# Unread products of ones in TensorE's planned waits, and other prices in the planner, in a clustered attention and feed-forward kernel

## The chip, the cores and the metric

The kernel runs on one core of a Trainium2 chip. The metric is the device time of one execution in microseconds (us). Three executions before the change took 919.37, 920.08 and 920.59 us, so the median is 920.08 us.

## The reference

Inputs: `q`, `k`, `v` of shape (4 batches, 8 heads, 768 positions, 64), 16 centroids per head, `moe_w_in` (512 x 2048), `moe_w_out` (2048 x 512), all float32. For each batch and head every query and key is given to the centroid whose normalised product with it is largest; a query attends only to keys of its own cluster:

```
mask   = q_assign[:, :, :, None] == k_assign[:, :, None, :]
scores = where(mask, scale * q @ k.T, -1e9)
attn   = softmax(scores);  attn_out = attn @ v
x = attn_out as 3072 tokens x 512
h = x @ w_in
g = where(h >= 1, h, where(h <= -1, 0, (h + 1)**2 / 4))
out = g @ w_out                       # 3072 x 512
```

## The kernel before, in words

Float32 operands are scaled and split into two float16 parts (high and low), and a product is three float16 products (high by high, high by low, low by high). Heads go in pairs: `kv_load` brings q, k and v of a pair, `kv_scale`, `kq_split`, `v_split` and `assign` scale, split, transpose (by DMA) and find the clusters. A batch has three units of 256 query rows; for every unit and head pair there are four score tiles of 128 rows by 768 keys. `at_scores` makes one (8 matmuls of 384 columns) in a pair of PSUM banks, VectorE adds a term and takes the row minimum into `sS` and `sbi`, ScalarE takes the exponential (`at_soft`), and the result is split into high and low and transposed: early in the run, every second tile by 6 TensorE transposes against the identity `idf` (`by_tensor`), otherwise by GpSimd, ScalarE and a DMA transpose (`hl` to `pT`). `at_av` multiplies by v: 8 small and 36 large matmuls of 64 output rows in the bank `bank_a`, which only `at_av` writes; ScalarE copies one half of that bank, VectorE reads the other, and the unit's `x` results. `ffn1` (24 matmuls of 256 columns) and `ffn2` (12 of 512 columns) are the feed-forward part, for 8 slices of the hidden width. The two weight matrices are loaded, scaled and split in the first part of the run as well (`w_load`, `w_bits`, `w_sum`, `w_split`; `w_sum` is 8, or 4, matmuls with a tile of ones, `ones`).

What sets the order: nothing is issued while the program is described. A `Recorder` writes down every instruction as a node with its engine, its price in ns (`price`, line 76), the PSUM banks it touches and what it depends on. `issue` (line 277) then runs eight rounds of a list scheduler: `forward` (line 154) simulates all engines and the one DMA queue (SP's) with these prices, `backward` gives new priorities, and the round with the shortest simulated span is kept. The program is issued in that order, by the start time of the simulation, so each engine's instruction order, SP's queue of DMAs included, is that of the plan. On the chip each engine works through its own list in order and waits for what it depends on; the plan's times themselves are not enforced.

Two things in the prices matter here. TensorE's node costs are doubled for every start before `COLD` = 75e3 ns (line 217). And `price` gives a matmul of n columns n/2.4 + 2.5 ns; one with at most 64 output rows n/4.8 + 1.2 ns (`at_av`); a transpose counts twice its columns, so 128 columns are priced at 109 ns.

All instructions of the plan are issued from line 292, so the trace shows L292 everywhere and the tile's name tells what an instruction is.

Of the kernel before, what the change touches and what calls it, by code (L numbers as in the profile page):

```python
# [11 lines left out]
F32 = mybir.dt.float32  # L12
# [15 lines left out]


LATENCY = dict(tensor=280, scalar=252, vector=230, gpsimd=175)  # L30
COLD, AHEAD = 75e3, 1500

LOOK, MARGIN = 0.4, 4000
ROUNDS = 8
# [3 lines left out]
class Recorder:  # L38
# [37 lines left out]
    def price(self, eng, op, out, ins, kw):  # L76

        if "dma" in op:
            n = 1
            for k in out.shape:  # L80
                n *= k
            kb = n * mybir.dt.size(out.dtype) / 1024

            return 33, 79.0 if kb == 2 else kb, "transpose" in op
        n = max(self.free(a) for a in [out] + ins[:1])
        ps = any(a.space == PSUM for a in ins)
        cols = sum(isinstance(kw.get(k), bass.AP) for k in ("scale", "bias", "scalar", "scalar1", "scalar2"))
        if eng == "tensor":
            n = self.free(ins[1])
            half = self.free(ins[0]) <= 64 and n > 100  # L90
            if op == "transpose":
                n *= 2
            elif ins[1].dtype == F32:
                n *= 4
            return n / 4.8 + 1.2 if half else max(n / 2.4 + 2.5, 24)
        if eng == "scalar":
            cols += kw.get("accum_out") is not None
            first = n == 1 and kw.get("scale") == 0.0
            return 93 + n / 1.2 + 94 * cols - 43 * ps + 1283 * first
        if eng == "vector":  # L100
            wide = [a for a in ins if self.free(a) > 1 or n == 1]
            wait = 400 if not ps and (len(wide) > 1 or op in ("tensor_scalar", "tensor_copy")) else 0
            fast = 1
            if op in ("tensor_scalar", "tensor_copy") and not ps:
                fast = 4 if mybir.dt.size(out.dtype) == 2 and mybir.dt.size(ins[0].dtype) == 2 and n > 64 else 2
            return 68 + n / 0.96 / fast + 61 * cols + 20 * (op == "reciprocal") + wait
        return 55 + n * (2.03 if op == "tensor_tensor" else 0.9 if op == "memset" else 3.5)
# [46 lines left out]
    def forward(self, prio):  # L154

        clock, ready, avail = {}, {}, {}
        left = {x: len(x.preds) for x in self.nodes}
        at = dict.fromkeys(self.nodes, 0.0)
        for x in self.nodes:
            if not x.preds:  # L160
                heappush(ready.setdefault(x.eng, []), (0.0, prio[x], x.i))
        hw, ring, sent, span = 450.0, 0.0, [], 0.0
        self.order, bank = [], {}
        todo = len(self.nodes)
        while todo:
            todo -= 1
            best = None
            for e, q in ready.items():
                now = clock.get(e, 0.0)
                a = avail.setdefault(e, [])  # L170
                while q and q[0][0] <= now:
                    _, s, i = heappop(q)
                    heappush(a, (s, i))
                t = now if a else q[0][0] if q else None
                if t is not None and (best is None or t < best[0]):
                    best = t, e
            t, e = best
            q = ready[e]
            while q and q[0][0] <= t:
                _, s, i = heappop(q)  # L180
                heappush(avail[e], (s, i))
            pick = heappop(avail[e])
            x = self.nodes[pick[1]]

            more = [(s, r, i) for r, s, i in q[:8] if r < t + x.cost * LOOK and s < pick[0] - MARGIN]
            if more:
                heappush(avail[e], pick)
                _, t, i = min(more)
                q.remove((t, prio[self.nodes[i]], i))
                heapify(q)  # L190
                x = self.nodes[i]

            free = max((until for k in x.banks for o, until in bank.get(k, {}).items() if o != e), default=0.0)
            if free > t:
                clock[e] = t
                heappush(q, (free, prio[x], x.i))
                todo += 1
                continue
            if x.dma and x.dma[0] > 256 and ring > t + AHEAD:

                clock[e] = t
                heappush(q, (ring - AHEAD, prio[x], x.i))
                todo += 1
                continue
            if x.dma:
                kb, tr = x.dma
                t = max(t, hw, sent[-8] if len(sent) > 7 else 0.0)
                clock[e] = t + x.cost
                hw = t + (650 if tr else 475)
                ring = max(ring, hw + (650 if tr else 784)) + kb * (5.6 if tr else 3.25)  # L210
                if tr:

                    hw = max(hw, ring - 1000)
                end = ring + (400 if tr else 1300)
                sent.append(end)
            else:
                clock[e] = t + x.cost * (2 if e == "tensor" and t < COLD else 1)
                end = clock[e] + LATENCY[e]
            for k in x.banks:
                bank.setdefault(k, {})[e] = end  # L220
            x.start, x.busy = t, clock[e]
            span = max(span, end)
            self.order.append(x)
            for y in x.succs:
                raw = x.dma or x.eng != y.eng or (y.preds[x] and x.eng != "tensor")
                at[y] = max(at[y], end if raw else x.busy)
                left[y] -= 1
                if not left[y]:
                    heappush(ready.setdefault(y.eng, []), (at[y], prio[y], y.i))
        return span  # L230
# [43 lines left out]
                    heappush(ready.setdefault("sync" if p.dma else p.eng, []), (at[p], -prio[p], -p.i))  # L274
        return start

    def issue(self):
        for x in self.nodes:
            for y in x.preds:
                y.succs.append(x)  # L280
        prio = {x: x.step for x in self.nodes}
        best = None
        for _ in range(ROUNDS):
            span = self.forward(prio)
            if best is None or span < best[0]:
                best = span, self.order
            prio = self.backward({x: x.start for x in self.nodes})
        span, self.order = best
        with self.tc.manual_schedule():
            for x in self.order:  # L290
                for fn, args, kw in x.calls:
                    fn(*args, **kw)  # L292

# [57 lines left out]
def tile_clustered_attention_moe(  # L351
# [10 lines left out]
    nc = tc.nc  # L362
# [6 lines left out]
    P = 128  # L369
# [21 lines left out]
    rec = Recorder(tc)  # L391
# [30 lines left out]
    bank = [psum.tile([P, 1024], F32, name=f"bank{i}") for i in range(3)]  # L422
    bank_a, bank_h = [psum.tile([P, 512], F32, name=f"bank{x}") for x in "ah"]
# [30 lines left out]
    ones = const.tile([P, P], BF16, name="ones")  # L454
# [618 lines left out]
    for s in sorted(ev):  # L1073
        rec.step = s
        for fn, args in ev[s]:
            fn(*args)
    rec.issue()


# [30 lines left out]
```

## Time and profile before

| | |
|---|---|
| median of 3 executions | 920.08 us (919.37 to 920.59) |
| profiled execution | 923.2 us, span from first to last instruction 921.4 us |
| mean granted TensorE clock | 0.981 of full speed |
| busy share of the span: TensorE, VectorE, ScalarE, GpSimd | 88%, 66%, 75%, 61% |

The profile follows one execution. PE is TensorE, DVE VectorE, ACT ScalarE, POOL GpSimd, SPq the DMA queue of SyncE. A busy share is an average over stages that have different limits, so the rows below are cut by stage. [...] The length of a group of matmuls includes the time in which the last one drains.

### The profile page before, as it was taken

How to read it: one execution, taken by the hardware profiler on the slowest of the kernel's cores; microseconds unless marked ns; L12 is line 12 of the kernel's file. 1: busy time of each engine (PE TensorE's matmuls, PEld its weight loads, DVE VectorE, ACT ScalarE, POOL GpSimd, SP SyncE). 2: the span in 40 equal slices, each digit the busy share in tenths (PEclk: the TensorE clock that was granted, in tenths of full speed). 3: DMA queues.
4: the chain of work that ended last, by engine and by line, in shares of the span. 5: the costliest groups of instructions: out<-in, count | busy, mean ns of one | idle time of the engine just before them, and what ended most of it. 6: DMA issues, size and time to landing. Idle time of an engine off the chain costs nothing.

```text
span 921.4 us, 19471 instructions
## 1 busy us (share of the span) xinstructions
PE 812.9 (88%) x7414; PEld 559.2 (61%) x7414; DVE 604.1 (66%) x1322; ACT 691.6 (75%) x1173; POOL 565.6 (61%) x520
## 2 busy tenths in 40 slices
PE   0256668988998999999989999998998999999998
PEld 0234446655766766676666666766666666666664
DVE  5998777887888565646776665547886555554222
ACT  6989997977778677778868778777887677777232
POOL 1766786975565577765555667655656677666221
PEclk9998789999999999999999999999999999999999
DMA  9979956796899958978999778888899768576100
GB/s 293 251 176 218 238 127 145 155 188 139 200 179 159 189 109 144 181 130 193 196 186 163 147 150 166 149 175 170 184 179 174 136 136 129 108 130 113 19 24 24
DMA packets 409535, 144.39 MB, mean 157 GB/s; under 512 B 386272, under 2 KB 401632, under 8 KB 409440
## 3 DMA queue, kind: packets, MB, share of 16 engines
q1 hardware_dynamic: 409440, 143.14, 77.0%
q8 instruction: 58, 0.95, 0.4%
q14 instruction: 37, 0.30, 0.1%
HBM read 40.40 MB, written 6.29 MB: 51 GB/s over the span
## 4 chain that ended last, share of the span: by engine, by line
PE 65%; DVE 10%; ACT 6%; issue 5%; POOL 3%; ACTq 0%; DVEq 0%; POOLq 0%
PE bank L292 47%; PE banka L292 10%; PE bankh L292 8%; DVE sS L292 3%; DVE r L292 2%; ACT sS L292 2%; DVE bank L292 2%; POOL hl L292 1%; ACT w L292 1%; DVE bankh L292 1%; DVE mx L292 1%; ACT hl L292 1%; POOL g L292 1%; ACT r L292 1%; DVE n L292 0%
## 5 line engine op out<-in xcount | busy, mean ns | idle before, releaser
L292 POOL TENSOR_TENSOR hl<-sS,hl 128x768 f16<-128x768 f32 x181 | 303.9, 1683 | 148.7 <-ACT hl L292 115.9
L292 PE MATMUL bank<-w,g 128*128 128x512 f16 x1152 | 271.1, 379 | 0.3 <-POOL g L292 0.2
L292 PEld LDWEIGHTS <-w 128*128 128x128 f16 x2304 | 224.4, 98 | 66.8 <-issue 23.0
L292 DVE CUSTOM_DVE_ANT_0 sS<-bank,zero,er 128x768 f32<-128x768 f32 x192 | 194.3, 1012 | 97.7 <-PE bank L292 67.8
L292 PEld LDWEIGHTS <-kvq 128*64 128x64 f16 (+1 forms) x3264 | 191.1, 106 | 86.2 <-issue 41.3
L292 ACT ACTIVATE sS<-sS,sbi 128x768 f32<-128x768 f32 x192 | 179.2, 933 | 83.9 <-DVE sbi L292 80.2
L292 POOL TENSOR_TENSOR g<-r,g 128x512 f16<-128x512 f32 x96 | 112.6, 1173 | 122.8 <-ACT g L292 119.2
L292 PEld LDWEIGHTS <-g 128*128 128x128 f16 x1152 | 110.7, 98 | 119.1 <-issue 2.1
L292 PE MATMUL bank<-kvq 128*128 128x384 f16 x768 | 162.4, 336 | 19.3 <-DVE sbi L292 14.1
L292 ACT CAST hl<-sS 128x768 f16<-128x768 f32 x181 | 148.3, 825 | 4.9 <-DMA pT<-hl 3.7
L292 PE MATMUL bank<-x,w 128*128 128x256 f16 x1032 | 123.9, 272 | 10.5 <-DVE r L292 5.2
L292 ACT ACTIVATE r<-r,f_ra,f_rs 128x512 f32<-128x512 f32 x96 | 77.8, 810 | 70.7 <-DVE r L292 69.7
L292 PE MATMUL banka<-pT,kvq 128*64 128x256 f16 x1728 | 106.4, 279 | 0.0
L292 DVE TENSOR_SCALAR r<-bank,f_lo,f_hi 128x512 f32<-128x512 f32 x64 | 51.6, 807 | 51.0 <-PE bank L292 41.9
L292 POOL TENSOR_TENSOR w<-w 128x1024 f32<-128x1024 f32 (+1 forms) x28 | 59.8, 2143 | 33.9 <-ACT w L292 32.0
L292 ACT CAST g<-r 128x512 f16<-128x512 f32 x96 | 58.8, 612 | 25.2 <-DVE r L292 18.7
L292 DVE SCALAR_TENSOR_TENSOR r<-bank,f_gs,r 128x512 f32<-128x512 f32 x64 | 47.9, 749 | 24.3 <-ACT r L292 15.6
L292 PE MATMUL bank<-wk,w 128*128 128x256 f16 x504 | 61.1, 272 | 3.1 <-DVE bank L292 2.1
L292 PE MATMUL bankh<-x,w 128*128 128x256 f16 x504 | 60.1, 273 | 2.2 <-DVE r L292 2.0
L292 PEld LDWEIGHTS <-ones 128*128 128x128 bf16 x244 | 17.2, 107 | 53.5 <-issue 38.5
L292 DVE TENSOR_SCALAR r<-bankh,f_lo,f_hi 128x512 f32<-128x512 f32 x32 | 25.8, 806 | 25.4 <-PE bankh L292 19.8
L292 ACT ACTIVATE n<-kvq,sc 128x768 f16<-128x768 f32 x42 | 37.1, 924 | 1.7 <-DVE sc L292 1.6
(158 smaller groups left out, 842.5 us busy)
## 6 DMA issues: line engine op xcount, KB each, us to landing
w<-in_moe_w_in_dram SPq DMA_DIRECT2D x14, 512.0 KB, 4.8
w<-in_moe_w_out_dram SPq DMA_DIRECT2D x14, 512.0 KB, 4.7
kvq<-in_k_dram SPq DMA_DIRECT2D x16, 384.0 KB, 3.6
kvq<-in_q_dram SPq DMA_DIRECT2D x16, 384.0 KB, 3.8
kvq<-in_v_dram SPq DMA_DIRECT2D x16, 384.0 KB, 4.1
out_dram<-o SPq DMA_DIRECT2D x11, 512.0 KB, 3.0
o<-in_v_dram SPq DMA_DIRECT2D x8, 384.0 KB, 3.7
pT<-hl SPq DMA_TRANSPOSE x181, 4.0
```

What stands on the lines that cost most here:

```text
L292: fn(*args, **kw)
```

## The change

TensorE's price is doubled only for starts before 15 us instead of 75 us. The price of a 64-row matmul rises from n/4.8 + 1.2 to n/4.8 + 9 ns. A transpose of a float32 tile now counts four times its columns (216 ns for 128 columns instead of 109 ns). The scheduler is otherwise the same, so it plans the whole program anew with these prices.

When the planned order is issued, `issue` walks through it and, ahead of a TensorE node whose planned start is more than 600 ns after the planned end of the TensorE node before it, puts in as many extra matmuls as fit in the planned wait at 217 ns each. Such a matmul multiplies `ones` by `ones`, read four times to make 512 columns, and writes all of `bank_a`. This is done from 10 us to 300 us of planned time, and not while results in `bank_a` have readers that come later in the order, nor before the planned end of the last such reader. Nothing reads what the extra matmuls write. They depend on nothing but `ones` and the earlier users of `bank_a`.

```diff
-COLD, AHEAD = 75e3, 1500
+COLD, AHEAD = 15e3, 1500
+WARM, PAUSE, FILL = (10e3, 300e3), 600, 217
...
-            if op == "transpose":
-                n *= 2
-            elif ins[1].dtype == F32:
+            if ins[1].dtype == F32:
                 n *= 4
-            return n / 4.8 + 1.2 if half else max(n / 2.4 + 2.5, 24)
+            return n / 4.8 + 9 if half else max(n / 2.4 + 2.5, 24)
...
-            self.order.append(x)
+            self.order.append((x, t, x.busy))
...
-    def issue(self):
+    def issue(self, idle, bank):
...
-            for x in self.order:
+            done, free, unread = 0.0, 0.0, set()
+            for x, start, busy in self.order:
+                own = any(name == bank for name, _ in x.banks)
+                if x.eng == "tensor":
+                    t = max(done, free, WARM[0])
+                    while not unread and start < WARM[1] and t + FILL < start and start - done > PAUSE:
+                        idle()
+                        t += FILL
+                    done = busy
+                    if own:
+                        unread = {y for y in x.succs if y.eng != "tensor" and any(name == bank for name, _ in y.banks)}
+                elif own:
+                    unread.discard(x)
+                    free = max(free, busy + LATENCY[x.eng])
                 for fn, args, kw in x.calls:
                     fn(*args, **kw)
...
-    rec.issue()
+    still = ones.unsqueeze(1).to_broadcast([P, 4, P])
+    rec.issue(lambda: nc.tensor.matmul(bank_a, ones, still, start=True, stop=True), bank_a.tensor.name)
```

## Rows read from the trace of the kernel before

**Rows 1.** Each stretch: busy us (x instructions) per engine, PEclk, DMA share, GB/s
```profile
15.00:62.00 47.00, 15.56 (x181) 11.59 (x180) 43.46 (x93) 38.11 (x44) 29.32 (x18) 1.00 0.94 255
62.00:140.00 78.00, 49.33 (x467) 33.81 (x465) 63.08 (x160) 73.59 (x110) 56.70 (x45) 0.80 0.82 188
140.00:300.00 160.00, 146.15 (x1375) 100.73 (x1374) 132.09 (x313) 130.23 (x232) 105.83 (x95) 1.00 0.83 167
300.00:880.00 580.00, 566.27 (x5169) 390.55 (x5167) 348.36 (x729) 428.64 (x759) 363.74 (x332) 1.00 0.79 150
```
**Rows 2.** The same view in stretches of 4 us
```profile
72.00:76.00 4.00, 2.04 (x8) 0.74 (x6) 3.96 (x10) 3.69 (x6) 3.92 (x5) 0.78 0.77 157
84.00:88.00 4.00, 2.54 (x62) 2.41 (x63) 3.09 (x11) 3.98 (x6) 1.39 (x4) 1.00 1.53 186
96.00:100.00 4.00, 4.00 (x41) 3.17 (x41) 1.98 (x3) 4.00 (x8) 3.96 (x3) 0.50 0.31 63
```
**Rows 3.** TensorE in order of time: start, us, instruction, count [idle before <-releaser]
```profile
14.50 1.01 PE L292 MATMUL bank<-wk,ones 128*128 128x128 bf16 x8 [7.74 <-DVE wk L292]
...
54.05 1.49 PE L292 MATMUL bank<-kvq 128*128 128x384 f16 x4
...
70.43 2.72 PE L292 MATMUL bank<-kvq 128*128 128x384 f16 x8
73.57 0.89 PE L292 MATMUL bank<-kvq 128*128 128x384 f16 x4 [0.42 <-DVE sbi L292]
...
78.09 3.36 PE L292 MATMUL banka<-pT,kvq 128*64 128x256 f16 x36
...
85.10 0.87 PE L292 MATMUL bank<-idf,sS 128*128 128x128 f32 x6 [2.29 <-ACT sS L292]
...
93.61 0.86 PE L292 MATMUL bank<-kvq 128*128 128x384 f16 x4 [2.98 <-DVE sbi L292]
95.00 1.54 PE L292 MATMUL bank<-idf,sS 128*128 128x128 f32 x6 [0.53 <-ACT sS L292]
...
96.90 4.05 PE L292 MATMUL banka<-pT,kvq 128*64 128x256 f16 x36
```
**Rows 4.** ScalarE's waits, 15 to 140 us: total us, times, longest
```profile
ACT sS L292 <- DVE sbi L292: 5.8, 6, 2.8
...
ACT w L292 <- DVE w_sw L292: 1.2, 1, 1.2
ACT wk L292 <- DVE bank L292: 0.5, 1, 0.5
```
**Rows 5.** ScalarE in order of time, instructions that waited
```profile
56.56 0.93 ACT L292 ACTIVATE sS<-sS,sbi 128x768 f32<-128x768 f32 x1 [2.85 <-DVE sbi L292]
...
84.02 0.93 ACT L292 ACTIVATE sS<-sS,sbi 128x768 f32<-128x768 f32 x1 [1.03 <-DVE sbi L292]
...
102.99 0.94 ACT L292 ACTIVATE sS<-sS,sbi 128x768 f32<-128x768 f32 x1 [1.16 <-DVE sbi L292]
```
**Rows 6.** VectorE in order of time, the instructions before those
```profile
53.58 2.02 DVE L292 SCALAR_TENSOR_TENSOR w<-w,wk 128x1024 uint32<-128x1024 uint32 x1
55.52 1.00 DVE L292 CUSTOM_DVE_ANT_0 sS<-bank,zero,er 128x768 f32<-128x768 f32 x1
...
82.96 1.02 DVE L292 CUSTOM_DVE_ANT_0 sS<-bank,zero,er 128x768 f32<-128x768 f32 x1 [1.61 <-PE bank L292]
...
101.93 1.02 DVE L292 CUSTOM_DVE_ANT_0 sS<-bank,zero,er 128x768 f32<-128x768 f32 x1 [2.54 <-PE bankh L292]
```
**Rows 7.** TensorE in order of time, after 140 us
```profile
163.94 2.13 PE L292 MATMUL banka<-pT,kvq 128*64 128x256 f16 x36
166.00 0.82 PE L292 MATMUL bank<-kvq 128*128 128x384 f16 x4
...
188.13 0.39 PE L292 MATMUL bank<-wk,ones 128*128 128x128 bf16 x4 [2.07 <-DVE wk L292]
...
201.66 1.46 PE L292 MATMUL bank<-w,g 128*128 128x512 f16 x6
```

## The prediction, made before the result was known

> **What bounds the kernel now.** I first read the busy shares by stage [rows 1]. From 140 us on TensorE is the bound: it is busy 146.15 of 160 us and then 566.27 of 580 us, and idle for only 13.85 and 13.73 us. Before 140 us it is not. From 15 to 62 us VectorE works 43.46 of 47 us with the DMA engines at 0.94, and TensorE 15.56 us. From 62 to 140 us ScalarE works 73.59 of 78 us and TensorE 49.33 us, at a mean granted clock of 0.80. So the end comes when the TensorE work that is left at 140 us is done, and the first stage decides how much is left.
>
> The second view is the clock in short stretches [rows 2] beside TensorE's groups in order of time [rows 3]. [...] Before 62 us the column says 1.00, but the durations contradict it: four score matmuls took 1.49 us at 54.05, and the same four 0.89 us at 73.57, after a stretch of unbroken matmuls from 70.43 to 73.15. The eight `w_sum` matmuls at 14.50 come after 7.74 us of idle and take 1.01 us. I read the stage up to 73 us as run at the lower level throughout, and 62 to 140 us as changing: 36 `at_av` matmuls took 3.36 us at 78.09 and 4.05 us at 96.90, the latter after an idle time of 2.98 us at 93.61 and then a short group, against 2.13 us at 163.94 [rows 3, 7].
>
> The third view is who waits on whom. In 15 to 140 us ScalarE's waits that can go back to TensorE are 5.8 us for `sbi`, 1.2 us for `w_sw` and 0.5 us for `bank`: 7.5 us [rows 4].
>
> **The change, part by part.** *How many fills.* They go where the plan has TensorE idle. If the plan's idle time is that of the trace, it is 31.44 us in 15 to 62 us, 28.67 us in 62 to 140 us and 13.85 us in 140 to 300 us [rows 1], 74 us. At 217 ns that is at most 341 matmuls; waits under 600 ns and the remainder of each wait get none, so I expect 200 to 330. The 217 ns is right at full clock: six 512-column matmuls take 1.46 us with their drain, 0.24 us each at most [rows 7]. Their loads of weights lie beside the matmuls, as the others' do. They issue no DMA.
>
> *The clock.* A wait filled with matmuls is not idle, so I expect the higher level from about 15 us to 300 us, apart from dips where the real wait is longer than the planned one. TensorE's own time falls by some 9 us in 62 to 140 us (at a mean clock of 0.80, 49.33 us of work is about 40 us at 1.00) and some 7 us before [rows 1]. Most of this lies beside other work: TensorE is idle there anyway, and ScalarE or VectorE set the pace. What counts is ScalarE's idle time that the low clock caused. Two places can be followed. VectorE's score pass at 82.96 waited 1.61 us for scores that stand behind the `at_av` of 3.36 us; at 2.13 us it ends 1.23 us earlier, and ScalarE's wait of 1.03 us at 84.02 goes [rows 3, 5, 6, 7]. The pass at 101.93 waited 2.54 us, behind transposes of 1.54 us (0.87 us at full clock at 85.10) and `at_av` of 4.05 us: 0.67 + 1.92 = 2.59 us come off, and ScalarE's wait of 1.16 us at 102.99 goes [rows 3, 5, 6]. That is 2.2 us. The rest of the `sbi` waits, 5.8 - 2.85 - 2.19 = 0.8 us, I let go too [rows 4, 5]: term A is -3.0 us. Its ends are 0 (ScalarE then waits for the next thing, its DMAs or GpSimd) and -7.5 us (all of rows 4).
>
> *The price before 75 us.* With TensorE planned at half the cost from 15 us on, score tiles are ready earlier in the plan. ScalarE's longest wait, 2.85 us at 56.56, is for a VectorE pass that began at 55.52 right behind a weight operation of 2.02 us, with no wait for TensorE [rows 5, 6]. Only another order can shorten that. With VectorE 92% busy and the DMA engines at 0.94 [rows 1] there is little room, and the SP queue's transposes and loads move along in the new order. Between 0 and -2.85 us I take -1 us, term B.
>
> *The prices of transposes and `at_av`.* A group of six transposes is now priced at 6 x 216 = 1.30 us, and took 0.87 us at the higher clock, 1.54 us at the lower, drain included [rows 3]: the new price is nearer to the lower level, which the fills are to remove. An `at_av`'s 36 matmuls were priced at 36 x 54.5 = 1.96 us and are now at 36 x 62.3 = 2.24 us; they took 2.06 us from their start to the next group's start [rows 7]. So the plan was 0.1 us short for each and is now 0.18 us long. Neither changes an instruction's duration; both change the order everywhere. No row shows the new order. As bounds I take all of TensorE's idle time in 300 to 880 us lost or doubled, 13.7 us either way [rows 1]; I take 0, as there is no sign, and keep half of the bound for the range.
>
> Six transposes took 0.87 us at 85.10, in a stretch granted 1.00, and 1.54 us at 95.00 [rows 2, 3]: they follow the clock. [...]
>
> *What the fills cost.* A fill is in TensorE's list ahead of the real work. If the data comes earlier, relative to TensorE, than planned, real work waits for up to the whole burst; and the fill waits for the readers of `bank_a` if these are late. Before 140 us TensorE has slack for that. After 140 us it has none: there up to 13.85 us of fills [rows 1] may stand where TensorE is not idle in the real run. The longest wait there, 2.07 us at 188.13, is for a weight tile on VectorE [rows 7], a wait of the kind that stays when TensorE gets faster. As TensorE's lag uses up the next wait, most of an overrun is given back. Between 0 and +13.85 us I take +1 us, term C.
>
> **The sum.** -3.0 - 1.0 + 0 + 1.0 = -3.0 us on the profiled execution: 923.2 - 3.0 = 920.2 us, in a span of 921.4 - 3.0 = 918.4 us. That execution lies 3.1 us above the median of 920.08 us, so on the median I predict 917.0 us.
>
> **The rivals.**
>
> Rival 1, no change: the low clock was hidden. For it: ScalarE is 94% busy in 62 to 140 us and VectorE 92% before [rows 1], so ScalarE's time saved at 84.02 and 102.99 could turn into waits for GpSimd and DMA. Against it: at both places the chain from the slow `at_av` to ScalarE has no other member than VectorE's pass. Price: 0, with C of about 1 us: 920 to 921 us.
>
> Rival 2, slower: fills in the place of work. After 140 us the planned waits and the real ones fall apart, and TensorE, the bound, does the fills on top of its work. For it: the plan is a simulation, its errors add up over 300 us, and a wait that is short of the planned one by half costs half its fills. Against it: the list order is the plan's, so a wait for VectorE or ScalarE recurs at the same place, and one unduly filled shortens the next. Half of the 13.85 us is +6.9 us, less the 4 us of A and B: +2.9 us, 923 us; all of it gives +9.9 us, 930 us. It decides from the point where more than 4.0 of the 13.85 us, some 18 of 64 fills, fall on time in which TensorE had work.
>
> Rival 3, slower by the order: the new plan adds waits of TensorE in 300 to 880 us. Half of the bound is +6.9 us, less 3.0: +3.9 us, 924 us. The same draw with the other sign gives 917.0 - 6.9 = 910 us, which belongs to "faster".
>
> Rival 4, the clock does not hold: the fills run at the lower level, each at twice its planned 217 ns, and every filled wait is overrun by its own length. The 31.44 us before 62 us [rows 1] would then be 63 us of fills beside 15.56 us of work in 47 us, up to 31 us late. Against it: the clock rose after the unbroken group at 70.43 [rows 3].
>
> **How the numbers follow.** A measurement of this kernel can tell about 0.2%, 1.8 us. Forecast, with its favourable draws of order: 0.53. Rival 1 and what ends within 1.8 us of before: 0.21. Rival 2: 0.14. Rival 3: 0.10. Rival 4: 0.02. So faster 0.53, same 0.21, slower 0.26. The forecast's own range is 908 to 918 us: its lower end is A and B at their far ends (917.0 - 4.5 - 1.85 = 910.7 us) with a small part of a better order. The range for 8 in 10 takes in rival 1 and most of rivals 2 and 3: 908 to 926 us.
>
> **What would show it.** Right: 200 to 330 matmuls `banka<-ones` from 10 to 300 us; four score matmuls before 62 us near 0.85 us and every `at_av` after 78 us near 2.1 us; a granted clock above 0.95 in 62 to 140 us; ScalarE's `sbi` waits before 140 us down from 5.8 to about 2 us; TensorE's own work, fills aside, reaching the same point 3 to 4 us earlier at 300 us. Wrong: score matmuls stay near 1.5 us (rival 4); ScalarE's idle time before 140 us unchanged with other releasers (rival 1); TensorE fuller than 146 us in 140 to 300 us with real work ending later there (rival 2); more idle time than 13.7 us after 300 us (rival 3).

## The result, and the profile after

The changed kernel takes 922.22 us (median of 7 executions, 921.88 to 924.74) against 920.08 us before (918.68 to 921.67). The ratio is 1.0030, with a 95% interval of 1.0016 to 1.0044: slower by 0.3%, where I had forecast faster by 0.3%. This ratio and those below are estimated from all executions of a set but one (of the kernel before, in the last set, 2148.87 us), so they can differ from the quotient of the medians, which is 1.0023 here. Its profiled execution took 922.06 us, in a span of 920.3 us.

The stages of the changed kernel, with the columns of [rows 1] (PEclk is TensorE's granted clock, with 1.00 for full speed):

```profile
15.00:62.00 47.00, 42.31 (x379) 23.51 (x379) 44.53 (x98) 41.62 (x51) 26.49 (x18) 1.00 1.06 259
62.00:140.00 78.00, 58.08 (x497) 36.19 (x496) 66.68 (x156) 72.91 (x107) 63.26 (x47) 0.86 0.78 178
140.00:300.00 160.00, 149.34 (x1400) 102.99 (x1399) 127.83 (x309) 129.53 (x228) 103.50 (x94) 0.99 0.84 170
300.00:880.00 580.00, 566.35 (x5172) 390.87 (x5169) 350.73 (x730) 430.48 (x759) 368.35 (x331) 1.00 0.79 149
```

TensorE is fuller in the first three stages, by 26.8, 8.8 and 3.2 us, and its busy time from 300 to 880 us is the same to 0.1 us. The fullness is fills:

```profile
L1094 PE MATMUL banka<-ones 128*128 128x512 bf16 x273 | 66.4, 390 | 3.2 <-DVE rb L308 3.1
```

There are 273 of them, within the 200 to 330 expected. To see past them I counted the other matmuls started by a given time and multiplied each kind by its spacing in the traces at a granted clock of 1.00 (163 ns for 384 columns, 108.7 for 256, 216.5 for 512, 57.2 for the large and 31 for the small ones of `at_av`, 110 for a transpose, 55.8 for 128 columns of `w_sum`, 25 for the smallest). By 140 us the kernel before has done 41.5 us of such work, the changed one 41.6 us; by 300 us it is 182.2 and 180.9 us. (I read nothing from differences under 0.5 us.) So by 140 us order and fills together had brought no work forward, and 1.3 us were lost between 140 and 300 us. (This is against one profile; a second one of the kernel before, below, stands at 42.8 and 184.9 us.)

The clock did come, but not everywhere I said. TensorE of the changed kernel in order of time, as in [rows 3]:

```profile
47.34 0.81 PE L308 MATMUL bank<-kvq 128*128 128x384 f16 x4
...
72.19 2.13 PE L308 MATMUL banka<-pT,kvq 128*64 128x256 f16 x36
...
86.23 1.01 PE L308 MATMUL bank<-wk,ones 128*128 128x128 bf16 x8 [4.33 <-DVE wk L308]
87.04 2.76 PE L308 MATMUL bank<-kvq 128*128 128x384 f16 x8
90.54 0.59 PE L1094 MATMUL banka<-ones 128*128 128x512 bf16 x1 [0.75 <-DVE rb L308]
...
134.89 1.01 PE L308 MATMUL bank<-wk,ones 128*128 128x128 bf16 x8 [2.90 <-DVE wk L308]
135.76 1.44 PE L308 MATMUL bank<-kvq 128*128 128x384 f16 x4
139.02 1.01 PE L1094 MATMUL banka<-ones 128*128 128x512 bf16 x2 [1.82 <-DVE rb L308]
...
141.67 2.67 PE L308 MATMUL banka<-pT,kvq 128*64 128x256 f16 x36
```

Score matmuls take 0.81 us for four already at 47 us (1.49 us before), and the first `at_av` 2.13 us (3.36 us before). But there are no fills from 72 to 90 us and from 124 to 139 us. An `at_av` has then left results in `bank_a`, and VectorE's pass over `rb`, their last reader, ends only at 90.5 and 139.0 us; until it has, no fill may be put in. The granted clock is 0.50 from 84 to 92 us and from 136 to 140 us:

```profile
84.00:88.00 4.00, 1.77 (x12) 1.25 (x12) 3.77 (x4) 4.00 (x6) 3.82 (x5) 0.50 0.87 180
...
136.00:140.00 4.00, 2.18 (x7) 0.91 (x6) 3.43 (x11) 2.71 (x5) 3.60 (x2) 0.50 0.01 2
```

Both times TensorE had been idle for 4.33 and 2.90 us just before or within the stretch. ScalarE's wait on `sbi` before 140 us, 5.8 us in [rows 4], is now

```profile
ACT sS L308 <- DVE sbi L308: 4.4, 4, 2.0
```

### The profile page after: what moved, and what is told of

The parts are those of the page before. It is cut to its first block, busy times and chain, and to the rows that moved or that the text cites. A ratio compares the mean times of both kernels' runs of the same rounds, so it can differ in the third digit from the quotient of the medians.

```text
span 920.3 us, 20021 instructions
## 1 busy us (share of the span) xinstructions
PE 857.8 (93%) x7687; PEld 578.3 (63%) x7687; DVE 607.6 (66%) x1322; ACT 693.5 (75%) x1173; POOL 571.6 (62%) x520
## 4 chain that ended last, share of the span: by engine, by line
PE 65%; DVE 9%; ACT 7%; POOL 6%; issue 5%; DMA 2%; ACTq 0%; POOLq 0%; DVEq 0%; SPq 0%
PE bank L308 49%; PE banka L308 9%; PE bankh L308 8%; POOL hl L308 2%; DVE r L308 2%; DVE sS L308 2%; ACT w L308 2%; POOL w L308 1%; ACT sS L308 1%; DMA pT<-hl 1%; ACT hl L308 1%; DVE wk L308 1%; POOL g L308 1%; DVE bank L308 1%; ACT wk L308 1%
## 5 line engine op out<-in xcount | busy, mean ns | idle before, releaser
L308 PEld LDWEIGHTS <-kvq 128*64 128x64 f16 (+1 forms) x3264 | 187.6, 104 | 75.0 <-issue 30.0
L308 POOL TENSOR_TENSOR g<-r,g 128x512 f16<-128x512 f32 x96 | 115.1, 1199 | 122.2 <-ACT g L308 122.1
L308 PE MATMUL bank<-kvq 128*128 128x384 f16 x768 | 158.2, 330 | 14.5 <-DVE sbi L308 8.9
L308 PE MATMUL banka<-pT,kvq 128*64 128x256 f16 x1728 | 103.0, 273 | 0.0
L1094 PE MATMUL banka<-ones 128*128 128x512 bf16 x273 | 66.4, 390 | 3.2 <-DVE rb L308 3.1
L1094 PEld LDWEIGHTS <-ones 128*128 128x128 bf16 x273 | 26.1, 99 | 37.1 <-issue 11.7
```

The lines of the kernel that those rows point to most:

```text
L1094: rec.issue(lambda: nc.tensor.matmul(bank_a, ones, still, start=True, stop=True), bank_a.tensor.name)
```

## The experiments

Ratios are against the kernel before, run on the same chip in the same rounds, with 95% intervals.

**Prices and fills apart.** The first four kernels. e1 is the changed kernel without fills, e2 the kernel before with fills, e3 the fills with one of the three prices, e4 a control: an irrelevant price moved by 0.1 ns.

```diff
# e1_prices_only, of the changed kernel
-WARM, PAUSE, FILL = (10e3, 300e3), 600, 217
+WARM, PAUSE, FILL = (0.0, 0.0), 600, 217
# e2_fills_only, of the changed kernel (e3_fills_cold: the same without the first pair)
-COLD, AHEAD = 15e3, 1500
+COLD, AHEAD = 75e3, 1500
-            if ins[1].dtype == F32:
+            if op == "transpose":
+                n *= 2
+            elif ins[1].dtype == F32:
-            return n / 4.8 + 9 if half else max(n / 2.4 + 2.5, 24)
+            return n / 4.8 + 1.2 if half else max(n / 2.4 + 2.5, 24)
# e4_nudge, of the kernel before
-            return n / 4.8 + 1.2 if half else max(n / 2.4 + 2.5, 24)
+            return n / 4.8 + 1.3 if half else max(n / 2.4 + 2.5, 24)
```

> The changed kernel's order on every engine, without its 273 fills. Theory O (the loss comes from the new order that the new prices draw; the fills give and take little): 922 to 924 us, TensorE at the lower clock up to about 70 us again, and the same TensorE work left at 300 us as in the changed kernel to about 1 us. Theory F (the new order is as good as the old or better, and the fills after 140 us, 22 of them or 4.8 us, stand in the way of work): 917 to 919 us. Theory C (the clock does help, and the order hides it): 925 us or more.

Measured: 921.61 us, 1.0014 [1.0004, 1.0023]. The new order alone costs a little.

> The three prices of the kernel before, so its order on every engine, with fills in that plan's waits (238 of them). Theory O: 919 to 920 us, no different from before, or a little faster if the clock is worth anything. Theory F: 922 to 925 us, with TensorE's real work ending later at 300 us. Theory C: 916 to 918 us, with ScalarE's waits at 84 and 103 us gone.

Measured: 924.96 us, 1.0046 [1.0034, 1.0057]. On the old order the fills cost 0.46%.

> The fills and the price up to 15 us as in the changed kernel; the prices of transposes and of the 64-row matmuls as before. Theory O: another draw, anywhere from 917 to 925 us. If the two prices left out here are what made the order worse: 917 to 920 us; if it is the price before 75 us: 922 us as the changed kernel.

Measured: 928.47 us, 1.0087 [1.0073, 1.0100], slower than any of the three ranges.

> The kernel before with one price moved by nothing that matters: 1.3 ns in place of 1.2 ns for a 64-row matmul; no fills. It is a control for how far the time moves when the planner only draws another order. Theory O needs it to move by about as much as the change did, 0.2 to 0.5% either way, though most likely slower: 920 to 924 us. Theories F and C expect 920 us within 0.1%.

Measured: 927.46 us, 1.0068 [1.0053, 1.0083]. The control moved by 0.68%, more than twice as far as the change, and beyond theory O's 924 us.

**Where the fills cost on the old order.** e2 has the instruction order of the kernel before on every engine, fills aside, so each of VectorE's 1322 instructions can be set against its counterpart. In e2 VectorE stood 0.3 us behind at 137 us and 4.2 us behind at 145 us. TensorE of e2 in between:

```profile
140.25 1.44 PE L310 MATMUL bank<-kvq 128*128 128x384 f16 x4 [1.00 <-DVE pT L310]
141.48 3.19 PE L1096 MATMUL banka<-ones 128*128 128x512 bf16 x7
144.47 2.25 PE L310 MATMUL bank<-x,w 128*128 128x256 f16 x12
```

Here seven fills, planned as 7 x 217 ns = 1.5 us, ran 3.0 us at the lower clock (0.50 in 140 to 144 us), and the first `ffn1` stood behind them. In the kernel before the same twelve matmuls follow the scores directly:

```profile
139.25 0.81 PE L292 MATMUL bank<-kvq 128*128 128x384 f16 x4 [0.25 <-DVE pT L292]
140.11 1.64 PE L292 MATMUL bank<-x,w 128*128 128x256 f16 x12
```

A second burst waited 2.72 us for the reader of its bank and then ran at the lower clock (0.64 in 104 to 108 us, 0.51 in 108 to 112 us), 11 fills in 4.85 us:

```profile
106.56 4.85 PE L1096 MATMUL banka<-ones 128*128 128x512 bf16 x11 [2.72 <-DVE rb L310]
```

So I cut the fills by planned time, keeping the order, and ran the price of e3 without fills:

```diff
# e5, of e2; e6 and e7 with 130e3 and 138e3
-WARM, PAUSE, FILL = (10e3, 300e3), 600, 217
+WARM, PAUSE, FILL = (10e3, 100e3), 600, 217
# e8_cold_no_fills, of the kernel before
-COLD, AHEAD = 75e3, 1500
+COLD, AHEAD = 15e3, 1500
```

> The order of the kernel before, with only the first 169 of the 238 fills: those that ran up to 96 us in the run with fills only. Theory B (two bursts did the harm there: the 11 fills that began at 106.56 us after a wait of 2.72 us for a reader of their bank, and the 7 that ran at the lower clock at 141.48 us): neither burst is there, the gain of 1.1 to 1.7 us that VectorE's instructions showed at 102 to 109 us is kept: 918.5 to 919.5 us. Theory H (the clock is hidden, whatever it gains by 109 us is waited off at ScalarE later): 920 us. Theory S (fills cost something spread over all bursts, 238 of them 4.2 us): 169/238 of it, 923 us.

Measured: 924.53 us, 1.0046 [1.0032, 1.0060].

> The same with the first 216 fills: the burst at 106.56 us is in, the 7 fills at 141.48 us and the 15 after them are out. Theory B: VectorE stands 0.3 us behind at 137 us and nothing is added: 920 to 920.5 us. Theory H: 920 us. Theory S: 216/238 of 4.2 us, 924 us.

Measured: 924.20 us, 1.0044 [1.0028, 1.0060].

> The same with the first 223 fills: the 7 at 141.48 us are back in, the last 15 are out. Theory B: the shift of VectorE's instructions jumps by 2.5 to 4 us between 137 and 145 us, and the time is 923 to 925 us, like all 238. If the last 15 did the harm after all: 920 to 921 us. Theory S: 924 us.

Measured: 925.29 us, 1.0055 [1.0037, 1.0073]. All three cost alike. Theory B, that two bursts did the harm, fell, and so did theory H's 920 us and theory S: 169 fills cost as much as 238.

> The kernel before with TensorE's doubled price ending at 15 us instead of 75 us and nothing else: no fills, the other prices as before. With the fills this order took 928.5 us. Theory O (the order that the prices draw sets the time): 926 to 929 us here too. Theory F (fills did it): 920 to 923 us.

Measured: 930.09 us, 1.0113 [1.0097, 1.0129]. That price alone, without a fill, costs no less than with fills (e3, 1.0087; the intervals just overlap): an order again. So fills do not cost the same on every order.

In e5 VectorE led the kernel before by 2.1 us at 110 us and by 1.7 us from 139 us on; between 181 and 192 us this turned into a lag of 1.4 us. The first 1.5 us went by 187 us, after ScalarE had waited 1.62 us at 177.72 for a DMA transpose, a wait that no profile of the kernel before has. The rest went from 188 us on. TensorE there:

```profile
187.92 0.39 PE L310 MATMUL bank<-wk,ones 128*128 128x128 bf16 x4 [1.99 <-DVE wk L310]
188.15 1.07 PE L310 MATMUL bank<-kvq 128*128 128x384 f16 x4
...
189.59 3.30 PE L310 MATMUL banka<-pT,kvq 128*64 128x256 f16 x36
```

After the wait for the weight tile, which stays at 1.99 us [rows 7 has 2.07 us before], the clock fell (0.57 in 188 to 192 us) in a stage where TensorE is the bound (in the kernel before it is busy 146.15 of 160 us [rows 1]). A fall between 136 and 196 us is in the profiles of e2, e5, e6 and e7 (in stretches of 4 us down to 0.50, 0.57, 0.64 and 0.50). The one profile of the kernel before has none there (1.00), but one at 460 to 470 us (0.83), and its time, 923.2 us, was 2.5 us above the median of the kernel before in this set (920.65 us). That put the comparison itself in doubt, so the next set has a second profile of the kernel before; e9, with the late fills back in; and two kernels (new order, old order) in which fills take a second bank, `bank_h`, when `bank_a` still has readers.

```diff
# e9_old_order_184, of e2
-                    while not unread and start < WARM[1] and t + FILL < start and start - done > PAUSE:
+                    while not unread and start < WARM[1] and not 100e3 < start < 138e3 and t + FILL < start and start - done > PAUSE:
# e10_two_banks_new, of the changed kernel; e11_two_banks_old, of e2. dead: those of the two
# banks whose last user in the order is not TensorE and whose next user is
-                    t = max(done, free, WARM[0])
-                    while not unread and start < WARM[1] and t + FILL < start and start - done > PAUSE:
-                        idle()
-                        t += FILL
+                    if dead:
+                        k = min(dead, key=lambda k: free[k])
+                        t = max(done, free[k], WARM[0])
+                        while start < WARM[1] and t + FILL < start and start - done > PAUSE:
+                            idle[k]()
+                            t += FILL
```

> The kernel before, unchanged, for a second profile. In the first one the granted clock fell at 460 to 470 us (0.83) and TensorE had done less by 400 us than in all the others; its time, 923.2 us, is 2.5 us above the median of its runs. Theory D (the clock falls now and then in the stage where TensorE is the bound, and each fall costs 1 to 3 us): this one has no fall there, or one elsewhere, and its time less 1 to 2 us for each fall is the same, about 920 us.

Measured: 919.01 us, a granted clock of 1.00 in 140 to 300 and in 300 to 880 us. It stands 2.5 us ahead of the first profile already at 109 us, and 4.2 us ahead after 470 us.

> The order of the kernel before with the first 169 fills and the last 15 of the 238, without the bursts in between (the one that waited at 106.56 us, the 7 at 141.48 us). With the first 169 alone VectorE was 2.1 us early until 182 us and lost 1.9 us at 188 us, where the clock fell while TensorE waited for a weight tile; the last 15 fills stand there. Theory D: the clock holds at 188 us, the 2.1 us stay: 918 to 919.5 us. Theory H (time won before 140 us is waited off later whatever the clock does): 920 to 921 us. Theory S (each fill costs its share): 923 us.

Measured: 922.50 us, 1.0020 [1.0008, 1.0032], 2 us better than e5. The late fills are worth something, as theory D has it, but the 918 to 919.5 us did not come: the lead on which I built it was mostly a lead over the first profile. Against the second, VectorE of e9 leads by only 0.8 us at 179 us, and is 0.7 us behind from 187 us on, after the same wait of ScalarE for a DMA transpose (1.60 us at 176.48).

> The changed kernel with a second bank for the fills: where results in the first bank are still to be read, they go to bank h when that is free; 334 fills in place of 273. In the changed kernel the clock fell at 86 to 94 us and at 131 to 143 us, both while a result in the fills' bank waited for its reader and no fill could be put in. Theory U (this blocking is why the clock was not held, and the fall at 131 to 143 us costs about 1 us where TensorE becomes the bound): no fall at 86 and at 140 us, 36 matmuls of at_av at 141 us in 2.1 us in place of 2.67: 920.5 to 921.5 us. Theory H: clock held and the time the same, 922 us. Theory S (more fills, more cost): 923 us or more.

Measured: 921.92 us, 1.0016 [1.0005, 1.0027]. The clock is 1.00 in every stage before 300 us, so the blocking was what had let it fall. `at_av` at 139.79 takes 2.13 us in place of 2.67. But the time is that of the same order without fills (e1), as theory H has it.

> The same second bank with the order of the kernel before: 279 fills in place of 238. Theory U: no fall of the clock at 72 to 76, 84 to 94, 104 to 111 and 140 to 146 us, no jump of VectorE's instructions between 137 and 145 us, where the one-bank version lost 2.5 to 4 us: 919 to 921 us against 925 us. Theory H: 924 to 925 us. Theory S: 925 us or more.

Measured: 923.03 us, 1.0022 [1.0012, 1.0032], 2 us better than e2, though the clock was not held here: it was 0.96 in 15 to 62 us, 0.64 in 64 to 68, 0.71 and 0.50 in 72 to 80 and 0.55 and 0.59 in 104 to 112 us, and VectorE was 2.7 us behind the second profile of the kernel before already at 40 us. Theory U is not shown by it.

e10 against e1 is the cleanest test of the forecast: one order, without fills and with 334 fills that hold the clock (in two sets, with medians of 920.73 and 920.75 us for the kernel before). It gives the clock's gain and the fills' cost together. The stage of 62 to 140 us, first e1, then e10:

```profile
62.00:140.00 78.00, 47.20 (x418) 31.42 (x417) 66.29 (x156) 72.42 (x107) 63.71 (x50) 0.74 0.79 180
```

```profile
62.00:140.00 78.00, 67.41 (x573) 40.30 (x573) 67.37 (x156) 73.32 (x108) 64.70 (x50) 1.00 0.80 178
```

and ScalarE's waits on `sbi` in 15 to 140 us, e1 and e10:

```profile
ACT sS L308 <- DVE sbi L308: 3.5, 4, 1.4
```

```profile
ACT sS L320 <- DVE sbi L320: 3.4, 3, 2.0
```

The mean clock goes from 0.74 to 1.00, and the total of the wait that was to shrink goes from 3.5 to 3.4 us.

**An exchange behind this total.** e1's four waits on `sbi` (0.57 us at 46.70, 0.81 at 69.35, 0.70 at 89.01, 1.38 at 137.65) are 0, 0.71, 0 and 0.76 us in e10: 2.0 us less. But e10 has a new one of 1.96 us, where e1 has none. The place in e1, then in e10:

```profile
52.95 0.68 DVE L308 TENSOR_SCALAR wk<-wk 128x1024 uint32<-128x1024 uint32 x1
...
53.27 2.35 POOL L308 TENSOR_TENSOR w<-w 128x1024 f16<-128x1024 f32 x1 [2.23 <-ACT w L308]
...
54.84 0.93 ACT L308 ACTIVATE sS<-sS,sbi 128x768 f32<-128x768 f32 x1
```

```profile
51.51 2.12 POOL L320 TENSOR_TENSOR w<-w 128x1024 f16<-128x1024 f32 x1 [1.62 <-ACT w L320]
...
51.81 2.38 DVE L320 TENSOR_SCALAR wk<-wk 128x1024 uint32<-128x1024 uint32 x1
...
55.15 0.94 ACT L320 ACTIVATE sS<-sS,sbi 128x768 f32<-128x768 f32 x1 [1.96 <-DVE sbi L320]
```

VectorE's weight operation `wk` takes 0.68 us where it begins 0.32 us ahead of GpSimd's `w`, and 2.38 us where it begins 0.30 us behind it; the score pass that ScalarE waits for stands behind it. Instruction by instruction against e1, ScalarE of e10 gains 0.6 us from 32 to 52 us, loses 2.1 us between 52 and 56 us, and gains 1.7 us from there to 214 us. The second profile of e10 (below) has 0.6, 2.1 and 1.9 us. So the fills and their clock were worth some 2.4 us, and this one place took 2.1 us back. Both profiles of the changed kernel lose the same 2.1 us there; after it, with the clock falling twice (to 0.50 in 84 to 88 and in 136 to 140 us in both), one gains 0.4 us and the other loses 0.2 us.

On the old order the fills bring about the same thing earlier. The second profile of the kernel before, then e9:

```profile
23.89 0.84 DVE L292 TENSOR_SCALAR wk<-wk 128x1024 uint32<-128x1024 uint32 x1
...
24.15 2.33 POOL L292 TENSOR_TENSOR w<-w 128x1024 f32<-128x1024 f32 x1
```

```profile
20.70 1.89 PE L1096 MATMUL banka<-ones 128*128 128x512 bf16 x8
...
22.66 0.37 DVE L310 TENSOR_SCALAR bank<-bank 128x2 uint32<-128x2 uint32 x2 [0.82 <-PE bank L310]
...
23.59 1.88 POOL L310 TENSOR_TENSOR w<-w 128x1024 f32<-128x1024 f32 x1
...
24.15 1.88 DVE L310 TENSOR_SCALAR wk<-wk 128x1024 uint32<-128x1024 uint32 x1
```

Eight fills stand ahead of a small matmul, VectorE waits for it, and its `wk` falls behind GpSimd's `w`. This is so in all six profiles with fills on that order (e2, e5, e6, e7, e9, e11), and in each ScalarE loses 1.1 us against the second profile of the kernel before between 18 and 36 us. No run moves `wk` ahead of `w` again with the fills in place, so what that would give is not shown.

**How far an order moves the time, and second profiles.** The last set: two more controls, which set the 64-row price of the kernel before to 1.4 and 1.1 ns in place of 1.2 ns, and e10 and the changed kernel once more, unchanged.

> The kernel before with the 64-row price at 1.4 ns in place of 1.2 ns, no fills: a second draw of the order. Theory O (the order that a price draws moves the time by more than the change did): anywhere from 920 to 928 us, and not within 1 us of both 920.7 us (before) and 927.5 us (the draw with 1.3 ns). If order hardly matters and the first draw was odd: 920 to 921.5 us.

Measured: 936.73 us, 1.0175 [1.0159, 1.0192], beyond theory O's 928 us.

> The same with 1.1 ns: a third draw. Theory O: 920 to 928 us. If order hardly matters: 920 to 921.5 us.

Measured: 932.52 us, 1.0132 [1.0114, 1.0150], beyond it too.

> The kernel with two banks for the fills, unchanged, for a second profile and one more time. If the typical execution lacks the clock: a fall of the granted clock somewhere in 62 to 500 us, and a time of 921.5 to 922.5 us. If it lacks the lead for another reason: a clock of 1.00 throughout, a time of 921.5 to 922.5 us, and VectorE less than 1 us ahead of the order without fills at 162 us. If the first profile was typical after all: 920 us.

Measured: 922.27 us, clock 1.00 up to 210 us and 0.84 in 210 to 220 us. VectorE is 0 to 0.8 us behind e1 at 105 to 120 us, where the first profile was 0.4 to 1.1 us ahead, 0.4 us ahead at 148 to 158 us, and 0.6 to 0.8 us behind after the fall. Both reasons hold: the lead was less (1.1 us of the difference from the first profile is there at 32 us already), and a fall of the clock took it.

> The changed kernel, unchanged, for a second profile. Falls of the clock again at 86 to 94 and at 131 to 143 us, where results in the fills' bank wait for their readers; 922 us with VectorE within 1 us of the order without fills from 114 us on.

Measured: 923.78 us. The clock falls at 80 to 92 and 132 to 144 us as in the first profile (to 0.50 in 84 to 88 and in 136 to 140 us), and once more at 300 to 310 us (0.83). It took 1.8 us more than expected, and VectorE is up to 1.2 us behind the order without fills by 146 us.

Orders and the work that they have done by 300 us, counted as above, with the time of the same profiled execution:

```
                      64-row price, COLD    us       work by 140, 300 us
before                1.2 ns, 75 us      923.2       41.5  182.2
before, second        1.2 ns, 75 us      919.0       42.8  184.9
e1 (new prices)       9 ns, 15 us        921.8       42.2  181.1
e10, e10 again        9 ns, 15 us        920.2, 922.3  42.6, 42.2  182.6, 180.6
changed, second       9 ns, 15 us        922.1, 923.8  41.6, 41.7  180.9, 180.4
e4                    1.3 ns, 75 us      926.7       40.4  177.8
e13                   1.1 ns, 75 us      932.5       40.4  175.5
e8                    1.2 ns, 15 us      931.4       36.5  173.5
e12                   1.4 ns, 75 us      937.8       39.7  172.9
```

Time and work by 300 us add up to 1103 to 1105 us in all but the last and e13 (1111 and 1108 us). So most of each difference between orders is made before 300 us; the two profiles of the kernel before, one order, differ by 2.7 us in this work.

## Why the prediction was wrong

The range held the time; the forecast of a gain did not hold. The median moved by +2.1 us where -3.0 us was forecast. Some 1.3 us of this is the order that the new prices draw (e1), where term B and the zero for the other prices came to -1.0 us. The rest, too small to tell from zero, lies in terms A and C, which came to -2.0 us.

*"What counts is ScalarE's idle time that the low clock caused ... That is 2.2 us ... term A is -3.0 us."* This step failed, twice over. First, one of its two waits was one execution's. In the second profile of the kernel before VectorE's two passes stand as follows

```profile
81.83 1.02 DVE L292 CUSTOM_DVE_ANT_0 sS<-bank,zero,er 128x768 f32<-128x768 f32 x1 [1.50 <-PE bank L292]
...
99.20 1.02 DVE L292 CUSTOM_DVE_ANT_0 sS<-bank,zero,er 128x768 f32<-128x768 f32 x1 [1.01 <-PE bankh L292]
```

(1.61 and 2.54 us of wait in [rows 6]). After the first ScalarE still waits 0.88 us, and after the second not at all: 1.16 us of the 2.2 us [rows 5] are not a property of the kernel. The wait after the first pass did go where I said: no profile with fills on the old order has it.

Second, I took every wait that ends as time gained and did not ask what meets what when engines move by a few tenths of a microsecond. In e10, with the clock held, the fills and the clock together brought ScalarE some 2.4 us, near the size of term A, and 2.1 us of it went where VectorE's `wk` fell behind GpSimd's `w`. Terms A and C together were forecast at -2.0 us and measured at 0.2 us, give or take 1.3 us (e10 against e1: 1.0016 and 1.0014). Rival 1 had the outcome, no gain. Its reason, that ScalarE's saved time turns into waits for GpSimd and DMA, holds in part: on the new order it turned into a wait for VectorE beside GpSimd, in e5 and e9 into 1.6 us of wait for a DMA transpose.

*"I expect the higher level from about 15 us to 300 us, apart from dips"* was right before 62 us (four score matmuls 0.81 us at 47.34) and wrong after: the mean granted clock was 0.86 in 62 to 140 us, not above 0.95. e10, whose fills have a second bank (1.00 in that stage), shows that the condition on unread results did this. I had read the condition on unread results in the diff and not asked how long `rb` stays unread, which the trace could have told.

*"No row shows the new order ... I take 0, as there is no sign."* Failed as to size and place. I bounded this term by TensorE's idle time after 300 us, but the order acts before. The new prices' order costs 0.4 to 2.1 us (e1's interval). The other four draws were slower by 6.3 (e4), 10.4 (e8), 12.2 (e13) and 16.1 us (e12), by their ratios. All five draws lie on the slower side, so a new order had to be counted as a loss and not as 0. Why they do was not tested; that the old prices may have been picked because their order was fast is an untested rival.

*Term C, +1 us for the fills.* The sign was right on the old order: there they cost 0.2 to 0.55%, and bursts that ran at the lower clock (0.50 to 0.64) or waited for their bank's reader (rivals 2 and 4 in small) were seen in e2; after the two bursts ScalarE was 2.4 and 2.5 us later. Removing those bursts did not remove the cost (e5, e6), as other losses were there: the 1.1 us before 36 us in every one of these kernels, the wait for a DMA transpose in e5, and falls of the clock at 188 to 196 us in e5, e6 and e7 (down to 0.57, 0.74 and 0.57), after each of which ScalarE is 1.3 to 1.6 us later. e9, which fills the wait at 188 us, is 2 us better than e5. These are readings of one profile each. On the new order the fills add nothing that can be told from e1 (1.0030 [1.0016, 1.0044] against 1.0014 [1.0004, 1.0023]).

Term B, -1 us for the price before 75 us: alone, this price costs 1.13% (e8). It was an order like the others, and I had priced it as a local gain.

What stays open: how the 0.3% divides between order and fills to better than 1 us; whether the 2.4 us would be kept with `wk` ahead of `w`; and how far e9's profile, the fastest of its 12 executions (919.70 us against a median of 922.50 us), stands for the others.

## What to carry to other kernels

Before a wait in one profiled execution is priced, take a second profile: here 1.16 of the 2.2 us foreseen at two waits were in the first only. A wait that ends is not yet time gained: here a held clock and its fills brought ScalarE some 2.4 us, and 2.1 us were lost where two operations of other engines changed places by 0.6 us. So follow a shift on to what the shifted operations meet next. Where a planner writes the whole order, changing a price is first of all drawing another order, and a control that moves a price by nothing shows what that is worth before any reason is believed.

## What had not been expected of the hardware

VectorE's weight operation (`wk<-wk`, 128 x 1024) took longer or shorter with what GpSimd was doing when it began. The 18 profiles have 252 of them. The 129 that begin with no TENSOR_TENSOR operation of GpSimd running take 0.67 to 0.91 us. The 123 that begin during one all end 0.5 to 1.1 us after it and take 0.69 to 2.75 us, 95 of them over 1 us. Why is not shown here.

The granted clock fell in single executions also in the stage where TensorE is busy 566.3 of 580 us (300 to 880 us): at 460 to 470 us (0.83) in one profile of the kernel before and not in the other, and at 300 to 310 us (0.83) in one of the changed kernel. In one of e10 it fell at 210 to 220 us (0.84). The two profiles of the kernel before, with the same instructions, differ by 4.2 us in all, 1.6 us of it at the fall. Transposes followed the clock here as well: six took 1.49 us at 90.92 us of the changed kernel, in a stretch granted 0.50, and 0.87 us at 98.56 us, in one granted 1.00.

```profile
90.92 1.49 PE L308 MATMUL bank<-idf,sS 128*128 128x128 f32 x6
...
98.56 0.87 PE L308 MATMUL bank<-idf,sS 128*128 128x128 f32 x6 [0.25 <-ACT sS L308]
```
